# Splitting seven of sixteen weight tiles inside the attention, and the rest on GpSimd over the first group

## The chip, the cores and the metric

One Trainium2 chip, one core. The metric is the device time of one execution in microseconds (us). Three runs of the kernel before gave 1213.04, 1215.56 and 1216.34 us; the median is 1215.56 us. A 0.3% difference is about 3.6 us.

## The reference

Two stages follow each other. The first is a linear attention: for each of 8 x 8 heads (576 tokens, 64 dimensions) queries and keys are projected to 128 features, the largest absolute value of each row is subtracted, and both exp(p) and exp(-p) are kept.

```
proj = x @ w_phi;  proj -= max(abs(proj), axis=-1);  phi = concat(exp(proj), exp(-proj))
kv = k_p^T v;  z = sum_s k_p;  out = (q_p kv) / (q_p z + 1e-6)
```

The second stage takes the 4608 tokens with 512 features each:

```
h = x @ w_in            # 512 -> 2048
g = h - tanh(h)
y = g @ w_out           # 2048 -> 512
```

The weights w_in and w_out arrive as 64-bit floating point numbers and are decoded on the chip to 32 bits.

## The kernel before, in words

**Attention.** A unit is a pair of heads of one batch; there are 32 units, u0 to u31. The loop `for i in range(NU + 2)` is a software pipeline: period i projects unit i (`project`, TensorE, with `m` and `t` on VectorE, L201 and L203), forms keys and queries of unit i-1 (`k_exp`, `q_exp` on ScalarE; `kv`, `ksum`, `qt`, `kv_turn` on TensorE), and forms the outputs of unit i-2 (`out_heads`, L267 and L278; `out_copy`; `den` reads the denominators back by DMA into `dn`; `den_recip` inverts them and sends them through memory to `rb`). `den_mul` (L314, GpSimd) multiplies unit i-3 by `rb` and stores it to memory as `xs`. In periods 0 to 31 one weight tile is decoded too (`dec_0` to `dec_2`, ScalarE and VectorE): tile n is w_in block n/2 for even n, w_out block n/2 for odd n. Within `tc.manual_schedule()` each engine keeps the order in which the lines are written.

**Weight splits.** TensorE multiplies in a reduced 32-bit format, so each weight tile (128x512) is split in a high part `wh` (a cast) and a low part `wl = w - wh` (a subtraction). `split_w(f)` does both for w_in block f (`whi`, `wli`) and w_out block f (`who`, `wlo`). The cast of w_in is on ScalarE (L88), that of w_out on VectorE (L90); the subtraction (L92) is on GpSimd, but for w_out blocks 3 to 15 on VectorE. Blocks 0 to 2 are split at the end of the attention (period 32 and after the loop), the others in steps 0 to 12 of the second stage. There, `pin` keeps instructions in the order in which they are written; the rest is ordered by a planner, which schedules everything outside the manual section.

**Second stage.** Tokens go in 12 groups of 384, and each group in 16 steps (f = 0 to 15), 192 steps in all. `stage1` makes h for one block of 128 features: 4 x 3 matmuls (`xh` by `whi`, `xl` by `whi`, `xh` by `wli`, L426) in one of three PSUM tiles `ph`. Five ScalarE functions and five VectorE operations (L442, L443, L445, L446, L447) make g; L447 frees `mk`, of which there is one buffer and which L441 of the next step writes. `split_g` makes `gh` (ScalarE, L453) and `gl` (GpSimd, L454). `stage2` of step f, written after `stage1` of step f+2, adds nine matmuls (L460, L461, L463) to three output tiles. The activations x of group 0 are loaded from `xs` in period 32 (`x_load`, four DMAs) and split there (`x_split`, four casts on ScalarE, four subtractions on VectorE, L109 and L110); those of group g+1 are loaded and split in steps 0 to 11 of group g. `den_mul` of the last unit is pinned on GpSimd in step 2. All DMAs are issued by SyncE's queue (SP), in order.

In `split_w` before, the engine of the subtraction and the early pool hang on these lines:

```
wh = (wpa if f < AHEAD else wp[0]).tile(...)      # AHEAD = 3
e = nc.vector if nm == "o" and f >= AHEAD else nc.gpsimd
```

Of the kernel before, what the change touches and what calls it, by code (L numbers as in the profile page):

```python
# [8 lines left out]
F32 = mybir.dt.float32  # L9
# [18 lines left out]
def f32(ap):  # L28
    return ap.bitcast(F32)
# [3 lines left out]
def tile_linear_attention_moe(  # L33
# [20 lines left out]
    NT = B * S // P  # L54
    TPP = 2 * S // P
    G = 3
    AHEAD = 3
    PC = 2 * S
    NCT = DM // P
    NF = DFF // P  # L60
# [18 lines left out]
    xp0 = ctx.enter_context(tc.tile_pool(name="xp0", bufs=1, reuse_waits="tile"))  # L79
    wi, wo, wp, xp = {}, {}, [], []  # L80

    def split_w(f, pin=lambda ins: ins):
        for d, nm in ((wi, "i"), (wo, "o")):
            w = d[f]
            wh = (wpa if f < AHEAD else wp[0]).tile([P, DM], F32R, name=f"wh{nm}{f}")
            wl = wpool.tile([P, DM], F32R, tag="w", name=f"wl{nm}{f}")
            if nm == "i":
                pin(nc.scalar.copy(wh, w))  # L88
            else:
                pin(nc.vector.tensor_copy(wh, w))  # L90
            e = nc.vector if nm == "o" and f >= AHEAD else nc.gpsimd
            pin(e.tensor_tensor(wl, w, f32(wh), ALU.subtract))  # L92
            d[f] = (wh, wl)

    def x_tiles(g):
        pool = xp0 if g % 2 == 0 else xp[0]
        xh = pool.tile([P, NCT, G * P], F32R, tag="xh", name=f"xh{g}")
        xl = pool.tile([P, NCT, G * P], F32R, tag="xl", name=f"xl{g}")
        return xh, xl, {}

    def x_load(g, xt, c):
        bp, o = divmod(g * G, TPP)
        x = xp0.tile([P, G * P], F32, tag="x", name=f"x{g}_{c}", bufs=4)
        nc.sync.dma_start(x, xs[bp][c, :, o * P : (o + G) * P])
        xt[2][c] = x
# [10 lines left out]
    with ExitStack() as c1:  # L116
# [15 lines left out]
        def warm(n):  # L132
            for _ in range(n):
                nc.tensor.matmul(pw[:, 0:256], zt[:, 0:P], zt, start=True, stop=True)
# [22 lines left out]
        def dec_0(u):  # L157
            rr = u.r.bitcast(U32).rearrange("p (n t) -> p n t", t=2)
            u.lo, u.hi = rr[:, :, 0], rr[:, :, 1]
            u.a = raw.tile([P, DM], U32, tag="dec_a", name=f"dec_a{u.nm}", bufs=2)  # L160
            nc.scalar.activation(f32(u.a), f32(u.hi), AF.Abs, scale=65536.0)
# [17 lines left out]
        def load(u):  # L179
            u.qk = p2.tile([P, PC], F32, tag="qk", name=f"qk{u.i}")  # L180
            w = PC if u.i else 3 * P
            for o in range(0, PC, w):
                nc.sync.dma_start(u.qk[:, o : o + w], qkT[u.i][:, o : o + w])

        def load_v(u):
            u.v = p2.tile([P, 5, 2, D], F32, tag="v", name=f"v{u.i}")
            nc.sync.dma_start(u.v.rearrange("p j e d -> p (j e d)"), v5[u.i])


        def project(u, r):  # L190
            pp = ps_pj.tile([P, 2, 512], F32, tag="pj", name=f"pp{u.i}_{r}")
            for a in range(3):
                j = 3 * r + a
                for e in range(2):
                    hs = slice(e * D, (e + 1) * D)
                    nc.tensor.matmul(  # L196
                        pp[:, e, a * F : (a + 1) * F], u.qk[hs, j * P : (j + 1) * P], wph[hs, :], start=True, stop=True
                    )
            x = pp[:, :, 0 : 3 * F].rearrange("p e (a f) -> p e a f", f=F)
            m = p2.tile([P, 2, 3], F32, tag="m", name=f"m{u.i}_{r}")  # L200
            nc.vector.tensor_reduce(m, x, AX.X, ALU.max, apply_absolute_value=True)  # L201
            t = p2.tile([P, 2, 3, F], F32, tag=f"t{r}", name=f"t{u.i}_{r}")
            nc.vector.tensor_tensor(t, x, m.unsqueeze(3).broadcast_to([P, 2, 3, F]), ALU.subtract)  # L203
            u.t[r] = t
# [22 lines left out]
        def k_exp(u, r):  # L227
            x, j0, j1 = (u.t[1][:, :, 1:3, :], 0, 2) if r == 1 else (u.t[2], 2, 5)
            for s in range(2):
                nc.scalar.activation(u.kp[:, :, j0:j1, s, :], x, AF.Exp, scale=1.0 - 2.0 * s)  # L230
# [62 lines left out]
        def den(u):  # L293
            w = 2 * S // P
            dn = tail.tile([P, w], F32, tag="dn", name=f"dn{u.i}")
            nc.sync.dma_start(dn, u.dd.rearrange("(n r) c -> n r c", r=32)[:, 0, :])
            u.dn = dn
# [33 lines left out]
        def unit(i):  # L331
            return units[i] if 0 <= i < NU else None


        with tc.manual_schedule():
            for i in range(NU + 2):
                a, c, p, p2_ = unit(i), unit(i - 1), unit(i - 2), unit(i - 3)
                if i + 1 < NU:
                    load(units[i + 1])
                    load_v(units[i + 1])  # L340
                if i == NU:
                    xt = {0: x_tiles(0)}
                    for j in range(NCT):
                        x_load(0, xt[0], j)
                if a:
                    a.kp = p2.tile([P, 2, 5, 2, F], F32, tag="kp", name=f"kp{i}")
                    if i == 0:
                        warm(16)
                    project(a, 0)
                if c and i < NU:  # L350
                    k_exp(c, 2)
                if p:
                    out_heads(p)
                if c and i == NU:
                    k_exp(c, 2)
                if 2 <= i < NU:
                    dec_0(dec[i])
                    dec_1(dec[i])
                if p:
                    out_copy(p)  # L360
                    den(p)
                if p2_:
                    den_mul(p2_)
                if i < 2:
                    warm(8)
                if c and i == 1:
                    kv(c)
                if a:
                    project(a, 1)
                if c and i > 1:  # L370
                    kv(c)
                if a:
                    k_exp(a, 1)
                if 2 <= i < NU:
                    dec_2(dec[i])
                if 2 <= i < NU - 2:
                    dec.append(dec_load(i + 2))
                if i == NU:
                    for j in range(NCT):
                        x_split(xt[0], j)  # L380
                if i == 0:
                    warm(8)
                if a:
                    project(a, 2)
                if i < 2:
                    dec_0(dec[i])
                    dec_1(dec[i])
                    dec_2(dec[i])
                    dec.append(dec_load(i + 2))
                if c:  # L390
                    c.qe = p1.tile([P, 2, 2, S], F32, tag="qe", name=f"qe{i - 1}")
                    pt = qt(c, 0)
                    q_exp(c, 0, pt)
                    ksum(c)
                    ptr = qt_rest(c)
                    kv_copy(c)
                    q_exp_rest(c, ptr)
                    pt = qt(c, 1)
                    kv_turn(c)
                    q_exp(c, 1, pt)  # L400
                if p:
                    den_recip(p)
                if i == NU:
                    split_w(0)
            for f in range(1, AHEAD):
                split_w(f)

    with ExitStack() as c2:  # L410
# [62 lines left out]

        NG = NT // G
        steps = [(g, f) for g in range(NG) for f in range(NF)]
        po, gs, gg = {}, {}, {}
        for i in range(len(steps) + 2):
            if i < len(steps):
                g, f = steps[i]
                if f == 0:  # L480
                    po[g] = [ps_o.tile([P, DM], F32, tag="o", name=f"po{g}_{t}") for t in range(G)]
                gs[i] = stage1(g, f, *xt[g][:2])
                if g + 1 < NG:
                    if f == 0:
                        xt[g + 1] = x_tiles(g + 1)
                    if f % 3 == 0 and f < 3 * NCT:
                        x_load(g + 1, xt[g + 1], f // 3)
                    if f % 3 == 2 and f < 3 * NCT:
                        x_split(xt[g + 1], f // 3, pin)
            if 1 <= i <= len(steps):  # L490
                g, f = steps[i - 1]
                gg[i - 1] = split_g(g, f, gs.pop(i - 1), G)
            if i == 2:
                den_mul(units[-1], pin)
            if i + AHEAD < NF:
                split_w(i + AHEAD, pin)
            if i >= 2:
                g, f = steps[i - 2]
                stage2(po[g], f, *gg.pop(i - 2), G)
                if f == NF - 1:  # L500
                    store(g * G, po.pop(g), G)
# [55 lines left out]
```

## Time and profile before

| | us |
|---|---|
| median of three runs | 1215.56 |
| profiled execution, its own time | 1214.86 |
| its span in the trace | 1213.1 |
| TensorE (PE) busy | 1186.4 (98%) |
| VectorE (DVE) busy | 890.8 (73%) |
| ScalarE (ACT) busy | 800.6 (66%) |
| GpSimd (POOL) busy | 272.6 (22%) |
| mean granted TensorE clock | 0.995 |

The span is the time between the first and the last instruction in the trace; 1.8 us of the execution's time lie around it. Busy shares are means over the whole span. The attention takes the first third of the span, the second stage the rest. PEclk is the granted TensorE clock as a share of 2.4 GHz.

### The profile page before, as it was taken

Reading aid. Unit: us, or ns where it says so; the run is one execution under the profiler, and the core shown is the slowest. Engines: PE = TensorE matmul, PEld = TensorE weight load, DVE = VectorE, ACT = ScalarE, POOL = GpSimd, SP = SyncE. Lnnn points to the kernel's source line nnn. Section 1 sums busy time; section 2 is a strip of 40 time slices with the busy share of each in tenths; the row PEclk is TensorE's granted clock in tenths of the full one; section 3 lists DMA queues with packets and bytes.
Section 4 is the critical chain, followed back from the end, with each engine's and each line's share of the span. In section 5 each row is a group of like instructions: output and inputs, shape, how many; then the busy total and the mean of one; then the engine's idle time right before and its main releaser. Section 6 shows DMA issues by size and latency. Waiting matters only on the chain.

```text
span 1213.1 us, 22447 instructions
## 1 busy us (share of the span) xinstructions
PE 1186.4 (98%) x8584; PEld 969.9 (80%) x8584; DVE 890.8 (73%) x1478; ACT 800.6 (66%) x1709; POOL 272.6 (22%) x253
## 2 busy tenths in 40 slices
PE   7999999999998899999999999999999999999998
PEld 5666666666665688999999999999999999999997
DVE  5877777777774998677677777777676777777665
ACT  3566566566666676777677766776676667766665
POOL 0001111011113552222222222222222222222222
PEclk9999999999999999999999999999999999999999
DMA  4566566556553000000010100010000100000000
GB/s 153 160 180 194 158 186 197 156 189 198 169 163 113 26 19 33 14 34 20 7 40 14 39 15 33 14 38 15 25 23 14 40 14 34 21 26 1 27 1 26
DMA packets 51180, 85.70 MB, mean 71 GB/s; under 512 B 13312, under 2 KB 28160, under 8 KB 51072
## 3 DMA queue, kind: packets, MB, share of 16 engines
q1 hardware_dynamic: 51072, 84.27, 22.6%
q8 instruction: 67, 1.10, 0.4%
q14 instruction: 41, 0.34, 0.1%
HBM read 65.08 MB, written 19.02 MB: 69 GB/s over the span
## 4 chain that ended last, share of the span: by engine, by line
PE 90%; DVE 5%; DMA 2%; issue 1%; ACT 1%; SPq 0%; DVEq 0%
PE ph L426 31%; PE po L461 10%; PE po L460 10%; PE po L463 10%; PE pp L196 7%; PE pc L238 6%; PE po L267 5%; PE pc L246 3%; PE ptt L209 3%; PE po L278 3%; DVE s L443 1%; PE ptk L257 1%; DVE s L447 1%; PE ptr L215 1%; DVE s L445 1%
## 5 line engine op out<-in xcount | busy, mean ns | idle before, releaser
L454 POOL TENSOR_TENSOR gl<-s,gh 128x384 fp32r<-128x384 f32 x192 | 197.5, 1029 | 592.6 <-ACT gh L453 582.0
L426 PE MATMUL ph<-xh,wli 128*128 128x384 f32 x768 | 259.8, 338 | 2.7 <-POOL wli L92 2.7
L426 PE MATMUL ph<-xh,whi 128*128 128x384 f32 x768 | 259.0, 337 | 1.0 <-DVE th L446 1.0
L426 PE MATMUL ph<-xl,whi 128*128 128x384 f32 x768 | 258.3, 336 | 0.0
L433 ACT ACTIVATE y<-ph 128x384 f32<-128x384 f32 x192 | 94.4, 491 | 228.4 <-PE ph L426 228.4
L460 PE MATMUL po<-who,gh 128*128 128x512 f32 x576 | 227.9, 396 | 7.9 <-ACT gh L453 7.8
L442 DVE SCALAR_TENSOR_TENSOR s<-s,y 128x384 f32<-128x384 f32 x192 | 111.1, 579 | 166.7 <-ACT s L435 166.6
L461 PE MATMUL po<-wlo,gh 128*128 128x512 f32 x576 | 227.0, 394 | 0.0
L463 PE MATMUL po<-who,gl 128*128 128x512 f32 x576 | 164.5, 394 | 0.0
L426 PEld LDWEIGHTS ph<-xh,whi 128*128 128x128 f32 x768 | 144.6, 188 | 10.1 <-issue 1.7
L447 DVE COPY_PREDICATED s<-mk,th 128x384 f32<-128x384 uint32 x192 | 136.4, 710 | 20.1 <-DVE th L446 0.5
L426 PEld LDWEIGHTS ph<-xl,whi 128*128 128x128 f32 x768 | 144.5, 188 | 8.2
L426 PEld LDWEIGHTS ph<-xh,wli 128*128 128x128 f32 x768 | 144.3, 188 | 3.8 <-POOL wli L92 3.6
L230 ACT ACTIVATE kp<-t 128x768 f32<-128x768 f32 (+1 forms) x128 | 87.2, 733 | 74.5 <-DVE t L203 74.5
L441 ACT ACTIVATE mk<-y,bias_t 128x384 f32<-128x384 f32 x192 | 117.9, 614 | 20.5 <-DVE s L447 20.5
L460 PEld LDWEIGHTS po<-who,gh 128*128 128x128 f32 x576 | 107.8, 187 | 28.6 <-ACT gh L453 11.5
L443 DVE SCALAR_TENSOR_TENSOR s<-s,s 128x384 f32<-128x384 f32 x192 | 115.1, 599 | 18.9 <-ACT mk L441 0.9
L463 PEld LDWEIGHTS po<-who,gl 128*128 128x128 f32 x576 | 108.5, 188 | 25.3
L201 DVE TENSOR_REDUCE m<-pp 128x6 f32<-128x768 f32 x96 | 91.8, 956 | 46.4 <-PE pp L196 46.4
L314 POOL TENSOR_TENSOR rb<-d,rb 128x576 f32<-128x576 f32 x32 | 46.5, 1454 | 336.6 <-DMA rb<-rr 336.6
L461 PEld LDWEIGHTS po<-wlo,gh 128*128 128x128 f32 x576 | 108.2, 188 | 16.4
L435 ACT ACTIVATE s<-y,bias_t 128x384 f32<-128x384 f32 x192 | 118.4, 617 | 0.0
(63 smaller groups left out, 1653.8 us busy)
## 6 DMA issues: line engine op xcount, KB each, us to landing
qk<-in_qkT SPq DMA_DIRECT2D x31, 576.0 KB, 4.7
v<-in_v SPq DMA_DIRECT2D x32, 320.0 KB, 7.0
rb<-rr SPq DMA_DIRECT2D x64, 144.0 KB, 2.9
xs<-rb SPq DMA_DIRECT2D x32, 288.0 KB, 2.4
x<-xs SPq DMA_DIRECT2D x48, 192.0 KB, 2.3
out<-o SPq DMA_DIRECT2D x36, 256.0 KB, 2.2
rawi<-in_moe_w_in SPq DMA_DIRECT2D x16, 512.0 KB, 4.3
rawo<-in_moe_w_out SPq DMA_DIRECT2D x16, 512.0 KB, 4.5
```

Source lines behind the costliest of these rows:

```text
L201: nc.vector.tensor_reduce(m, x, AX.X, ALU.max, apply_absolute_value=True)
L426: nc.tensor.matmul(h, wt[:, c * P : (c + 1) * P], x[:, c, 0:N], start=(i == 0), stop=(i == 3 * NCT - 1))
L433: nc.scalar.activation(y, h, AF.Square)
L435: nc.scalar.activation(s1, y, AF.Square, bias=bias_t[:, 0:1])
L441: nc.scalar.activation(mk, y, AF.Relu, bias=bias_t[:, 2:3])
L442: nc.vector.scalar_tensor_tensor(s1, s1, PC1, y, ALU.add, ALU.mult)
L443: nc.vector.scalar_tensor_tensor(s2, s2, PC2, s1, ALU.add, ALU.mult)
L447: nc.vector.copy_predicated(gs, mk.bitcast(U32), th)
L454: pin(nc.gpsimd.tensor_tensor(gl, gs, f32(gh), ALU.subtract))
L460: nc.tensor.matmul(po[t], a, wo[f][0], start=(f == 0), stop=False)
L461: nc.tensor.matmul(po[t], a, wo[f][1], start=False, stop=False)
L463: nc.tensor.matmul(po[t], gl[:, t * P : (t + 1) * P], wo[f][0], start=False, stop=(f == NF - 1))
```

## The change

`AHEAD` becomes 7. `split_w` now handles one tile n (even n: w_in, odd n: w_out). Tiles 0 to 13, that is blocks 0 to 6 of both weights, are split one per period in periods 1 to 14 of the attention, right after `den_mul`. The casts of these fourteen are on ScalarE, w_out's too. Tiles 14 to 31 are split in the first group, spread evenly over its 16 steps (1.2 per step); their casts stay where they were. Every subtraction is on GpSimd. The x of group 0 is loaded in period 30, ahead of that period's other DMAs except the loads of unit 31, and split at the end of period 31. The last period (33: outputs of u31, `den_mul` of u30) is no longer in the manual section and is ordered by the planner together with the second stage.

```
-    AHEAD = 3
+    AHEAD = 7
+    def split_w(n, pin=lambda ins: ins):
+        d, nm, f = (wi, wo)[n % 2], "io"[n % 2], n // 2
+        early = f < AHEAD
+        w = d[f]
+        wh = (wpa if early else wp[0]).tile([P, DM], F32R, name=f"wh{nm}{f}")
+        wl = wpool.tile([P, DM], F32R, tag="w", name=f"wl{nm}{f}")
+        if early or nm == "i":
+            pin(nc.scalar.copy(wh, w))
+        else:
+            pin(nc.vector.tensor_copy(wh, w))
+        pin(nc.gpsimd.tensor_tensor(wl, w, f32(wh), ALU.subtract))
+        d[f] = (wh, wl)
...
+        def period(i):
+            if i == NU - 2:
+                xt[0] = x_tiles(0)
+                for j in range(NCT):
+                    x_load(0, xt[0], j)
...
             if p2_:
                 den_mul(p2_)
+            if 1 <= i <= 2 * AHEAD:
+                split_w(i - 1)
...
             if p:
                 den_recip(p)
+            if i == NU - 1:
+                for j in range(NCT):
+                    x_split(xt[0], j)
...
         with tc.manual_schedule():
-            for i in range(NU + 2):
-                if i == NU:
-                    split_w(0)
-            for f in range(1, AHEAD):
-                split_w(f)
+            for i in range(NU + 1):
+                period(i)
+        period(NU + 1)
...
+        late = list(range(2 * AHEAD, 2 * NF))
+        NL = len(late)
-            if i + AHEAD < NF:
-                split_w(i + AHEAD, pin)
+            while late and late[0] <= 2 * AHEAD + i * NL // (NF - 1):
+                split_w(late.pop(0), pin)
```

## Rows read from the trace of the kernel before

**Rows 1.** Busy time per engine by stretch; then granted clock, DMA share, GB/s.
```profile
48.40:371.50 323.10, 322.08 (x4003) 206.66 (x4001) 250.63 (x369) 203.64 (x427) 40.82 (x29) 1.00 0.59 176
371.50:399.20 27.70, 22.33 (x180) 14.51 (x180) 12.62 (x23) 15.84 (x36) 12.28 (x9) 0.94 0.37 112
399.20:472.50 73.30, 65.53 (x308) 56.47 (x309) 68.81 (x108) 50.14 (x106) 37.83 (x29) 0.98 0.05 16
472.50:1199.10 726.60, 726.60 (x3645) 658.21 (x3644) 520.86 (x929) 505.76 (x1094) 176.12 (x174) 1.00 0.07 23
382.80:387.60 4.80, 4.80 (x32) 2.12 (x32) 0.51 (x3) 0.64 (x2) 2.49 (x2) 0.66 0.46 140
```
**Rows 2.** Waits of PE, 371 to 472.5 us: total, times, longest.
```profile
PE po L460 <- ACT gh L453: 7.0, 7, 1.7
PE ph L426 <- POOL wli L92: 2.7, 3, 1.3
PE ptt L209 <- ACT qe L220: 1.7, 1, 1.7
```
**Rows 3.** PE in order of time around the change of stage: start, us.
```profile
371.56 2.16 PE L267 MATMUL po<-qe,kv 128*64 128x288 f32 x16 [0.65 <-DVE kv L259]
...
382.79 3.77 PE L267 MATMUL po<-qe,kv 128*64 128x288 f32 x16 [0.65 <-DVE kv L259]
...
399.22 0.50 PE L460 MATMUL po<-who,gh 128*128 128x512 f32 x1 [0.36 <-ACT gh L453]
```
**Rows 4.** Groups of instructions, 416.8 to 462.4 us: count, busy, mean ns, idle.
```profile
L443 DVE SCALAR_TENSOR_TENSOR s<-s,s 128x384 f32<-128x384 f32 x9 | 11.3, 1261 | 0.6
...
L92 DVE TENSOR_TENSOR wlo<-wo,who 128x512 fp32r<-128x512 f32 x9 | 6.2, 688 | 0.2
...
L88 ACT CAST whi<-wi 128x512 fp32r<-128x512 f32 x8 | 4.9, 617 | 0.0
...
L90 DVE CAST who<-wo 128x512 fp32r<-128x512 f32 x9 | 3.8, 418 | 0.0
```
**Rows 5.** Groups of DVE and of POOL, 600 to 800 us.
```profile
L442 DVE SCALAR_TENSOR_TENSOR s<-s,y 128x384 f32<-128x384 f32 x48 | 26.9, 560 | 44.7 <-ACT s L435 44.7
L443 DVE SCALAR_TENSOR_TENSOR s<-s,s 128x384 f32<-128x384 f32 x48 | 26.8, 558 | 4.7
...
L454 POOL TENSOR_TENSOR gl<-s,gh 128x384 fp32r<-128x384 f32 x48 | 48.9, 1018 | 152.1 <-ACT gh L453 152.1
```
**Rows 6.** Lines L447 and L92: ns min/median/max, first and last start us.
```profile
L447 DVE COPY_PREDICATED s<-mk,th x10: 586/601/1533, 416.9 to 462.4; 128x384 f32<-128x384 uint32 x10
...
L92 POOL TENSOR_TENSOR wli<-wi,whi x16: 1266/1603/1626, 383.5 to 454.7; 128x512 fp32r<-128x512 f32 x16
```
**Rows 7.** POOL and DVE in order of time, one step of the first group.
```profile
459.56 1.25 POOL L454 TENSOR_TENSOR gl<-s,gh 128x384 fp32r<-128x384 f32 x1 [3.29 <-ACT gh L453]
...
460.04 1.19 DVE L443 SCALAR_TENSOR_TENSOR s<-s,s 128x384 f32<-128x384 f32 x1
```
**Rows 8.** Waits in the attention, 48.4 to 371.5 us.
```profile
ACT kp L230 <- DVE t L203: 52.9, 28, 1.9
...
DVE m L201 <- PE pp L196: 32.9, 53, 0.8
...
DVE rn L304 <- DMA dn<-dd: 0.8, 1, 0.8
```
**Rows 9.** Lines L203 and L171, all executions: ns min/median/max, first and last start.
```profile
L203 DVE TENSOR_TENSOR t<-pp,m x96: 956/957/958, 8.0 to 368.9; 128x768 f32<-128x768 f32 x96
...
L171 DVE SCALAR_TENSOR_TENSOR wi<-rawi,dec_ai x16: 679/682/1754, 17.3 to 355.0; 128x512 uint32<-128x512 uint32 x16
```
**Rows 10.** SP's queue in order of time: start, us.
```profile
374.48 2.00 SPq L104 DMA_DIRECT2D x<-xs  x4
...
392.61 1.10 SPq L309 DMA_DIRECT2D rb<-rr  x2
```
**Rows 11.** POOL in order of time: start, us.
```profile
405.23 1.43 POOL L314 TENSOR_TENSOR rb<-d,rb 128x576 f32<-128x576 f32 x1
```

More of the change, by code (lines that the diff above doesn't have):

```diff
@@ L80, in tile_linear_attention_moe @@
     wi, wo, wp, xp = {}, {}, [], []
[L82 to L93, printed above, removed]
+    def split_w(n, pin=lambda ins: ins):
[10 more added lines that the diff above has]
+        d[f] = (wh, wl)
     def x_tiles(g):
@@ L332, in unit @@
             return units[i] if 0 <= i < NU else None
-        with tc.manual_schedule():
-            for i in range(NU + 2):
[L337 to L340, printed above, removed]
-                if i == NU:
[L342 to L403, printed above, removed]
-                    split_w(0)
-            for f in range(1, AHEAD):
-                split_w(f)
@@ new lines, in period @@
+        def period(i):
+            a, c, p, p2_ = unit(i), unit(i - 1), unit(i - 2), unit(i - 3)
+            if i + 1 < NU:
+                load(units[i + 1])
+                load_v(units[i + 1])
+            if i == NU - 2:
+                xt[0] = x_tiles(0)
+                for j in range(NCT):
+                    x_load(0, xt[0], j)
+            if a:
+                a.kp = p2.tile([P, 2, 5, 2, F], F32, tag="kp", name=f"kp{i}")
+                if i == 0:
+                    warm(16)
+                project(a, 0)
+            if c:
+                k_exp(c, 2)
+            if p:
+                out_heads(p)
+            if 2 <= i < NU:
+                dec_0(dec[i])
+                dec_1(dec[i])
+            if p:
+                out_copy(p)
+                den(p)
+            if p2_:
+                den_mul(p2_)
+            if 1 <= i <= 2 * AHEAD:
+                split_w(i - 1)
+            if i < 2:
+                warm(8)
+            if c and i == 1:
+                kv(c)
+            if a:
+                project(a, 1)
+            if c and i > 1:
+                kv(c)
+            if a:
+                k_exp(a, 1)
+            if 2 <= i < NU:
+                dec_2(dec[i])
+            if 2 <= i < NU - 2:
+                dec.append(dec_load(i + 2))
+            if i == 0:
+                warm(8)
+            if a:
+                project(a, 2)
+            if i < 2:
+                dec_0(dec[i])
+                dec_1(dec[i])
+                dec_2(dec[i])
+                dec.append(dec_load(i + 2))
+            if c:
+                c.qe = p1.tile([P, 2, 2, S], F32, tag="qe", name=f"qe{i - 1}")
+                pt = qt(c, 0)
+                q_exp(c, 0, pt)
+                ksum(c)
+                ptr = qt_rest(c)
+                kv_copy(c)
+                q_exp_rest(c, ptr)
+                pt = qt(c, 1)
+                kv_turn(c)
+                q_exp(c, 1, pt)
+            if p:
+                den_recip(p)
+            if i == NU - 1:
+                for j in range(NCT):
+                    x_split(xt[0], j)
@@ L410, in tile_linear_attention_moe @@
+        xt = {}
+        with tc.manual_schedule():
+            for i in range(NU + 1):
+                period(i)
+        period(NU + 1)
     with ExitStack() as c2:
```

## The prediction

> **What bounds the kernel now.** First the busy time by stretch [rows 1]: TensorE (PE) is busy for 322.08 of 323.10 us of the attention and for all of 726.60 us after the first group. There only less matmul work would help, and the change removes none. The two stretches between are different: 5.4 us of PE idle from 371.5 to 399.2, and 7.8 us from 399.2 to 472.5, the 15 steps from the first second-stage product of step 0 to that of step 15. In the second, VectorE (DVE) is busy 68.81 of 73.30 us. That is 4.89 us a step; later PE takes 4.187 us (726.60 us for 3645 matmuls at 21 a step).
>
> Then the waits of PE [rows 2]: 7.0 us for `gh`, the end of the DVE chain; 2.7 us for `wli`, the early splits on GpSimd (POOL); 1.7 us for a `q_exp` that stands in ScalarE's (ACT) queue behind the casts of x. After that last idle time the clock falls: the granted clock from 382.8 to 387.6 us is 0.66 [rows 1], a mix of the two levels of 2.4 and 1.2 GHz, and the same 16 matmuls of `out_heads` take 3.77 us where they took 2.16 [rows 3], 1.6 us lost.
>
> Why DVE takes 4.89 us a step is seen in the groups and in the order of time. L443 takes 558 ns in the steady groups [rows 5] and 1261 ns in the first one [rows 4]; the single step shows it: `gl` runs on POOL from 459.56 to 460.81, L443 starts at 460.04 and ends at 461.23, 0.42 us after POOL is done [rows 7]. So a DVE operation that reads SBUF only waits until POOL's tensor operation ends. L203, with one input in PSUM, takes 956 to 958 ns in all 96 cases, with POOL or without [rows 9].
>
> **The change part by part.** I write times against the profiled execution, 1214.86 us.
>
> *Attention, splits of tiles 0 to 13.* Each period of 11.39 us (L203, 96 times from 8.0 to 368.9, three a period [rows 9]) gets one ACT cast of 0.617 us [rows 4] and one POOL subtraction of 1.27 to 1.6 us [rows 6]. The cast stands before `k_exp`, where ACT waits 1.9 us a period for `t` (52.9 us in 28 waits [rows 8]): hidden, and uncovered it would cost 14 x 0.617 = 8.6 us. POOL is busy 40.82 of 323.10 us [rows 1], so it has room; its operation falls behind `den_mul`, while DVE does `m` and `t` from PSUM, which L203 shows unharmed. DVE itself waits for PE 0.6 us at a time (32.9 us in 53 waits [rows 8]), so that small shifts are absorbed. I take 0, with a gain excluded, since PE has 1 us of idle there in all; the other end stands under the rivals.
>
> *x loaded in period 30.* Four DMAs take 2.00 us of SP's queue [rows 10]. Queued behind them now are `dn`, the store of `xs`, `rr` and `rb` of that period. DVE takes `dn` in order, and once waited 0.8 us for it [rows 8]; then `m` of the next unit and PE's projections follow. Bounds 0 and 2.0 us; I take +0.5, since the 0.6 us waits of DVE cover part. The `dn` DMA of period 32 goes out earlier by as much. The split at the end of period 31 lies where DVE has nothing else, and ACT's four casts end before `out_copy` of u30 needs it.
>
> *Transition, 371.56 to 399.22.* The 1.7 us wait of PE goes, since no cast of x stands in front of `q_exp`; with it I expect the slow clock to go, 1.6 us. The 2.7 us for `wli` go, as blocks 0 to 6 are split long before. The two waits of 0.65 us for `kv` stay [rows 3], though the planner may put first-stage matmuls into the second. Restarts of PE add some tenths. Sum -6.2 us, first `gh` product at about 393. What is late next is the chain of step 0 (ACT, DVE, `gh`). Bounds: -3.3 if that chain takes back the 2.7 us, -8 if the `kv` waits are filled too.
>
> *First group, 15 steps.* Count what POOL and DVE can't do at the same time. Per step before: L442 and L443 0.56 each, L447 0.60, the cast 0.42, `wlo` 0.69 on DVE; `gl` 1.02 and `wli` 1.27 on POOL [rows 4 to 6]; sum 5.12. DVE's pace was 45.5/9 = 5.06 us (ten L447 from 416.9 to 462.4 [rows 6]), so the sum holds within 1%. After: 0.56 + 0.56 + 0.60; 9 casts in 15 steps, 0.25; `gl` 1.02; 18 subtractions in 15 steps, 18 x 1.27/15 = 1.52. Sum 4.51, by the same 1% 4.46 us a step. That is still above PE's 4.187, so the first group stays bound by DVE and POOL: 15 x 4.46 = 66.9 in place of 73.3, -6.4 us. Bounds: -10.5 (4.187 a step, DVE keeps up because it starts a step ahead) and 0.
>
> *Added waits.* The cast of tile 14 writes memory that the attention's last tiles hold, as the cast of block 3 did. `den_mul` of u31 is pinned in step 2 with `gl` of steps 2 and on queued behind it, and PE behind them. Before, `rb` went out at 392.61 and POOL took it at 405.23 [rows 10, 11], over 11 us after; both move up by about 6 us, so the margin stays. The last period, now ordered by the planner, keeps its work; 0 to 2 us either way, inside the range.
>
> Sum: +0.5 - 6.2 - 6.4 = -12.1, so 1202.8 for an execution like the profiled one. That one lies 0.7 us under the median of 1215.56; I add a little and say **1203.0**.
>
> A rule speaks against the change. The Trainium skill (Perfetto Trace Analysis, section Optimizing Scalar/DVE Operations) says that moving operations between DVE and GpSimd might not help, as they share a read port of SBUF. By that rule the first group would gain nothing; it is the second rival. The trace agrees with the sharing [rows 7], and shows what the move costs: 1.27 us on POOL for 0.69 on DVE.
>
> **The rivals.**
>
> *PE becomes the bound (20%).* At 4.187 us a step the first group saves 10.5. For it: DVE's own work falls by 0.42 + 0.69 - 0.25 = 0.86 us a step, and the planner lets the first stage run up to three tiles ahead. Against: the sum above is a sum of things that exclude each other. 0.5 - 6.2 - 10.5 = -16.2: 1198.7.
>
> *The move gives nothing in the first group (16%).* Eighteen subtractions at 1.27 us are 22.9 us of POOL, against 13 x 1.27 + 13 x 0.69 = 25.5 us on both engines before. If POOL's longer holds, two in some steps, cost DVE what it no longer does itself, the step stays at 4.89. Against: four blocks are gone from the group, 4 x (0.42 + 0.69 + 1.27) = 9.5 us. +0.5 - 6.2: 1209.2.
>
> *Slower: the splits stall the attention (7%).* A POOL subtraction in each of 14 periods holds DVE just when `m` of the next projection is due. L171 shows the price: up to 1.75 us in place of 0.68 under `den_mul` [rows 9], 1.07 us. With POOL's slowest 1.6 us the hold is up to 1.6, less nothing if DVE's 0.6 us wait is already used: 14 x 1.6 = 22.4 us, 1214.86 + 22.4 - 12.1 = 1225. It turns the sign from 12.1/14 = 0.86 us of PE idle a period. Against: 29 `den_mul` in the attention's 323 us leave PE 1 us idle in all.
>
> *The change doesn't do what it says (5%).* The planner, free in the last period, puts `out_heads` and DVE's `dn` operations so that DVE stands in order before a DMA with step 0's chain behind it. Then the transition keeps its length and the first group starts late; the 6.2 are lost and the 6.4 stay: 1209.
>
> **How the numbers follow.** Forecast 52%, own range 1200 to 1206; rivals 20, 16, 7 and 5%. The range 1197 to 1209.5 holds the first, the forecast and most of the second, and leaves out the slower case; the transition's and the x loads' bounds (3 and 1.5 us up) lie inside. A change of 0.3%, 3.6 us, is about what a measurement of this kernel can tell from none. Faster by more 0.90, within 0.03, slower 0.07.
>
> **What would show it.** Right: no PE wait for `wli`, no wait of about 1.7 us for `q_exp` before `ptk` of u31, and a granted clock near 1.00 around `out_heads` of u31; L447 of the first group some 4.4 to 4.5 us apart; L443 still far above 558 ns there; L203 still 957 ns; the attention as long as before to within 1 us. Wrong: PE gaps in periods 1 to 14; a first group of 73 us; a first `gh` product later than 396. A clock that falls to half in the first group again would cost what the step's pace gains.

## The result and the profile after

The changed kernel took 1205.36 us in the median of six runs (1202.87 to 1206.69), the kernel before 1216.37 us on the same chip (1213.04 to 1217.57): a ratio of 0.991 (95% interval 0.9894 to 0.9926), 11.0 us less. The profiled execution took 1203.97 us, its span is 1202.0 us. The forecast for such an execution was 1202.8, the forecast time 1203.0.

The busy time by stretch of the changed kernel, cut where its own stages begin (columns as in rows 1; the last cut lies 0.5 us before its first product of step 15, at 461.50):

```profile
48.40:371.50 323.10, 322.21 (x4005) 206.80 (x4001) 252.13 (x368) 209.47 (x439) 56.63 (x41) 1.00 0.60 179
371.50:392.50 21.00, 20.18 (x182) 14.33 (x182) 8.35 (x18) 14.18 (x33) 4.14 (x3) 1.00 0.37 104
392.50:461.00 68.50, 63.36 (x304) 54.10 (x305) 61.45 (x89) 48.45 (x103) 43.20 (x34) 1.00 0.06 19
461.00:1188.00 727.00, 727.00 (x3647) 658.65 (x3646) 522.07 (x932) 505.72 (x1094) 177.07 (x174) 1.00 0.07 23
```

Against [rows 1], GpSimd (POOL) has 15.8 us more in the attention and TensorE (PE) is as busy there as before. The transition shrinks from 27.7 us to 21.0, at full clock. The first group still holds 5.1 us of PE idle; after it PE is busy without a gap. The same places in PE's order of time (compare [rows 3]):

```profile
363.45 0.94 PE L197 MATMUL pp<-wph,qk 64*128 64x128 f32 x12 [0.28 <-DVE t L204]
...
371.55 2.16 PE L268 MATMUL po<-qe,kv 128*64 128x288 f32 x16 [0.65 <-DVE kv L260]
...
381.05 2.16 PE L268 MATMUL po<-qe,kv 128*64 128x288 f32 x16 [0.65 <-DVE kv L260]
...
392.56 0.50 PE L462 MATMUL po<-who,gh 128*128 128x512 f32 x1 [0.18 <-ACT gh L455]
```

Period 32 starts its `out_heads` at 371.55, before at 371.56. The next `out_heads` takes 2.16 us where it took 3.77, and the first `gh` product comes at 392.56, where it came at 399.22. What PE waited for from 371 to 462 us (compare [rows 2]):

```profile
PE po L462 <- ACT gh L455: 2.3, 4, 0.8
PE po L465 <- POOL gl L456: 1.5, 3, 0.6
PE po L268 <- DVE kv L260: 1.3, 2, 0.7
PE ph L428 <- POOL wli L93: 1.3, 1, 1.3
```

7.0 us for `gh` became 2.3. The wait for `q_exp` is gone. Two waits are left on POOL: 1.5 us for `gl`, which wasn't there before, and one of 1.3 us for a `wli`. That one is the last w_in tile; in order of time, POOL and then PE:

```profile
449.60 1.33 POOL L456 TENSOR_TENSOR gl<-s,gh 128x384 fp32r<-128x384 f32 x1
450.90 1.26 POOL L93 TENSOR_TENSOR wli<-wi,whi 128x512 fp32r<-128x512 f32 x1
...
452.21 0.44 PE L428 MATMUL ph<-xh,wli 128*128 128x384 f32 x1 [1.29 <-POOL wli L93]
```

The even spread puts the last w_in tile in step 14, one step before its use, and PE stands until it is split. VectorE's (DVE) pace, by the operation that ends a step (L449, before L447, compare [rows 6]; minimum, median, maximum ns, first and last start):

```profile
L449 DVE COPY_PREDICATED s<-mk,th x15: 598/1394/1581, 390.5 to 451.2; 128x384 f32<-128x384 uint32 x15
```

Fourteen steps in 60.7 us are 4.34 us a step. The same fourteen steps before:

```profile
L447 DVE COPY_PREDICATED s<-mk,th x15: 579/602/1691, 396.4 to 465.2; 128x384 f32<-128x384 uint32 x15
```

They took 68.8 us, 4.91 a step; the 5.06 of the prediction is the pace of nine of them, from 416.9 to 462.4.

To compare the runs below I use three marks of each profile: T, the start of `out_heads` of period 32; G, the first `gh` product; S, the first copy of group 0's output (DVE), two us after the first product of step 15. What happens before T varies from profile to profile by up to 3.7 us, so T to S is the better measure. There is one profile of each kernel. Times are us, the ratios are to the kernel before on the same chip.

| kernel | T to G | G to S | T to S | ratio (95% interval) |
|---|---|---|---|---|
| before | 27.7 | 75.4 | 103.1 | 1 |
| changed | 21.0 | 71.0 | 92.0 | 0.991 (0.9894 to 0.9926) |
| late `wlo` on DVE | 21.0 | 73.9 | 94.9 | 0.9922 (0.9909 to 0.9934) |
| before, x alone | 25.1 | 75.4 | 100.5 | 0.9985 (0.9976 to 0.9994) |
| spread two earlier | 21.3 | 69.8 | 91.1 | 0.9912 (0.9897 to 0.9928) |
| no late subtractions | 20.8 | 64.9 | 85.7 | 0.9861 (0.9846 to 0.9876) |
| x back in period 32 | 22.6 | 72.2 | 94.8 | 0.9936 (0.9919 to 0.9953) |
| late `wlo` on DVE, two earlier | 21.3 | 72.2 | 93.5 | 0.9916 (0.99 to 0.9933) |
| late casts on ScalarE, two earlier | 21.8 | 67.2 | 89.0 | 0.9873 (0.9855 to 0.9891) |
| five early blocks | 21.0 | 78.9 | 99.9 | 0.9979 (0.9968 to 0.9989) |
| last period by hand | 21.0 | 71.1 | 92.1 | 0.9918 (0.9905 to 0.993) |
| late tiles in pairs | 21.0 | 74.2 | 95.2 | 0.994 (0.9927 to 0.9954) |
| five early, three earlier | 21.3 | 72.7 | 94.0 | 0.993 (0.9915 to 0.9944) |

T to S fell by 11.05 us from before to changed: all of the gain, 6.65 in the transition and 4.40 in the first group.

How far T to S varies between executions of one kernel isn't known; changed and last period by hand, which no mark tells apart, agree within 0.1 us. One thing does disturb it: for a stretch the granted clock falls to 0.50. Between T and S this happens twice in the profile of before (from 382.6 and from 416.6 us) and once in those of late `wlo` on DVE, x alone, x back, and five early, three earlier; in the others the clock stays at 1.00. Summed over windows of 0.4 us, each stretch costs PE 1.7 us of full-speed time. In the second one of before DVE was busy for 3.33 of 3.40 us (416.8 to 420.2), so it probably has no part in the 4.40 us; no run shows that. Whether a stretch belongs to the kernel or to the execution isn't shown: two of the changed kernel's six executions, the profiled one among them, have a mean granted clock of 0.997 or 0.998, the other four 0.995. Differences of 2 to 3 us between two profiles are read below with this in mind.

### The profile page after: what moved, and what is told of

It is laid out like the page before. It is cut to its first block, busy times and chain, and to the rows that moved or that the text cites. A ratio compares the mean times of both kernels' runs of the same rounds, so it can differ in the third digit from the quotient of the medians.

```text
span 1202.0 us, 22462 instructions
## 1 busy us (share of the span) xinstructions
PE 1181.3 (98%) x8584; PEld 967.1 (80%) x8584; DVE 881.3 (73%) x1458; ACT 804.7 (67%) x1716; POOL 288.8 (24%) x266
## 4 chain that ended last, share of the span: by engine, by line
PE 93%; DVE 3%; issue 1%; DMA 1%; POOL 0%; ACT 0%; DVEq 0%; SPq 0%; POOLq 0%; ACTq 0%
PE ph L428 32%; PE po L465 10%; PE po L463 10%; PE po L462 10%; PE pp L197 7%; PE pc L239 7%; PE po L268 5%; PE pc L247 4%; PE ptt L210 3%; PE po L279 3%; PE ptk L258 1%; DVE s L445 1%; PE ptr L216 1%; DVE s L449 1%; DMA dn<-dd 0%
## 5 line engine op out<-in xcount | busy, mean ns | idle before, releaser
L444 DVE SCALAR_TENSOR_TENSOR s<-s,y 128x384 f32<-128x384 f32 x192 | 108.0, 562 | 167.9 <-ACT s L437 167.9
L449 DVE COPY_PREDICATED s<-mk,th 128x384 f32<-128x384 uint32 x192 | 140.3, 731 | 20.5 <-ACT y L435 0.5
L462 PEld LDWEIGHTS po<-who,gh 128*128 128x128 f32 x576 | 107.9, 187 | 22.6 <-ACT gh L455 5.6
L443 ACT ACTIVATE mk<-y,bias_t 128x384 f32<-128x384 f32 x192 | 117.9, 614 | 6.5 <-DVE s L449 6.3
L439 ACT ACTIVATE s<-y,bias_t 128x384 f32<-128x384 f32 x192 | 117.6, 612 | 1.4 <-POOL gl L456 1.3
L437 ACT ACTIVATE s<-y,bias_t 128x384 f32<-128x384 f32 x192 | 118.4, 617 | 0.0
```

Of the source, the lines that this page charges most:

```text
L437: nc.scalar.activation(s1, y, AF.Square, bias=bias_t[:, 0:1])
L439: nc.scalar.activation(s2, y, AF.Square, bias=bias_t[:, 1:2])
L443: nc.scalar.activation(mk, y, AF.Relu, bias=bias_t[:, 2:3])
L444: nc.vector.scalar_tensor_tensor(s1, s1, PC1, y, ALU.add, ALU.mult)
L449: nc.vector.copy_predicated(gs, mk.bitcast(U32), th)
L462: nc.tensor.matmul(po[t], a, wo[f][0], start=(f == 0), stop=False)
```

## The experiments

**Late `wlo` back on VectorE.** The prediction added up the durations on DVE and POOL as if they excluded each other (below: the port sum). By that sum this is faster still.

```
-        pin(nc.gpsimd.tensor_tensor(wl, w, f32(wh), ALU.subtract))
+        e = nc.gpsimd if early or nm == "i" else nc.vector
+        pin(e.tensor_tensor(wl, w, f32(wh), ALU.subtract))
```

> The changed kernel, but the subtraction of the nine late w_out tiles is on VectorE again, as before the change. Theory (VectorE's operations on SBUF and GpSimd's exclude each other, and their sum sets the pace of the first group): the sum falls from 4.51 us a step by 9 x 1.27/15 = 0.76 and rises by 9 x 0.69/15 = 0.41, to 4.16, under TensorE's 4.187; the first group shrinks from 68.9 us to 63 to 65, and the time falls by 4 to 6 us against the changed kernel, to about 1200. Rival (VectorE's own work is the bound, so that the move to GpSimd is what brought the gain): VectorE gets 6.2 us more work in the group where it was busy for 61.5 of 68.5 us; the group is as long or longer, 68 to 72 us, and the time 1205 to 1209.

G to S grew by 2.9 us, from 71.0 to 73.9; 66 had been expected on this scale. The port sum fails. DVE's steps, as above:

```profile
L450 DVE COPY_PREDICATED s<-mk,th x15: 593/610/1607, 390.2 to 453.3; 128x384 f32<-128x384 uint32 x15
```

63.1/14 = 4.51 us a step, where the sum had said 4.16. The whole time isn't told apart from the changed kernel's (ratios 0.9922 and 0.991); the 4 to 6 us that the sum had promised are not there.

Not all of the 2.9 us is the move's. In both kernels PE waits 1.3 us for the last w_in tile and has no gap from there to S. This last piece, in the changed kernel and then in this one (columns as in rows 1):

```profile
452.21:463.58 11.37, 11.37 (x58) 10.37 (x58) 7.56 (x14) 7.46 (x17) 3.87 (x3) 1.00 0.00 1
```
```profile
453.30:466.20 12.90, 12.90 (x57) 11.91 (x58) 7.43 (x14) 7.45 (x17) 2.29 (x2) 0.87 0.01 1
```

The clock costs 1.5 us here. That leaves 1.4 us up to the end of that wait.

**x alone.** In the kernel before, the loads of x move to period 30 and the split to the end of period 31.

```
-                if i == NU:
+                if i == NU - 2:
                     xt = {0: x_tiles(0)}
...
-                if i == NU:
-                    for j in range(NCT):
-                        x_split(xt[0], j)
...
+                if i == NU - 1:
+                    for j in range(NCT):
+                        x_split(xt[0], j)
```

> The kernel before, with one part of the change alone: the first x loaded in period 30 and split at the end of period 31. Theory: the 1.7 us wait of TensorE for q_exp and the slow clock behind it (1.6 us) go, the x loads cost 0.4 us, the rest of the transition and the first group stay: 2.5 to 3.5 us faster than before, granted clock near 1.00 around the last out_heads. Rival (the waits for the early splits take it back, since GpSimd and ScalarE still have to split three blocks there): within 1 us of before, with the waits for wli grown from 2.7 us to over 5.

T to G fell by 2.6 us, and both effects of the theory are seen: the second `out_heads` takes 2.16 us, and no wait for `q_exp` is left. But the waits for `wli` grew from 2.7 to 3.5 us:

```profile
PE po L460 <- ACT gh L453: 7.0, 7, 1.7
PE ph L426 <- POOL wli L92: 3.5, 3, 1.7
```

The whole time fell by 0.15%, 1.8 us, less than expected; in the profile, PE also waited 1.0 us for `t` in the attention, behind the x loads. So of 6.65 us this part alone brings 2.6; the rest needs the early splits (the run with x back in period 32 has them without this part).

**The spread two tiles earlier.**

```
-            while late and late[0] <= 2 * AHEAD + i * NL // (NF - 1):
+            while late and late[0] <= 2 * AHEAD + 2 + i * NL // (NF - 1):
```

> The changed kernel, with the spread of the late tiles moved two tiles earlier, so that the last w_in tile is split in step 12 and not in step 14, one step before its use. Theory (the first group is 2 us longer than the 66.9 us of the sum because TensorE waits 1.29 us for the last wli, and step 14 behind it starts late): that wait goes, the pace of the other steps stays at 4.5, the group takes 66.5 to 67.5 us, the time falls by 1.5 to 2.4 us against the changed kernel. Rival (the pace of the port sets the end of the group whatever the order): the group stays at 68.5 to 69.5 and the time within 0.7 us.

The wait for `wli` is gone, and the stretch is 1.2 us shorter, T to S 0.9:

```profile
PE po L465 <- POOL gl L456: 2.8, 4, 1.4
PE po L462 <- ACT gh L455: 1.8, 2, 0.9
PE po L268 <- DVE kv L260: 1.3, 2, 0.7
```

The waits for `gl` grew from 1.5 to 2.8 us instead: with more tiles in the first steps POOL is late with `gl`. Between theory and rival; the times don't tell the two kernels apart.

**No late subtractions.**

```
+        if early:
+            wl = wpool.tile([P, DM], F32R, tag="w", name=f"wl{nm}{f}")
+        else:
+            wl = wh
...
-        pin(nc.gpsimd.tensor_tensor(wl, w, f32(wh), ALU.subtract))
+        if early:
+            pin(nc.gpsimd.tensor_tensor(wl, w, f32(wh), ALU.subtract))
```

> The changed kernel without the eighteen late subtractions: the low part of the late tiles is left out and their high part is used twice, so the matmuls stay. Theory (port sum): 4.51 - 1.52 = 2.99 us a step, under VectorE's own run of instructions and under TensorE's 4.187; TensorE is the bound, the first group takes 62.8 to 64 us, and the time falls by 5 to 6 us against the changed kernel. L443's counterpart (the second of the five operations) takes under 800 ns there. Rival (ScalarE and VectorE in turns, with one buffer for mk, set the pace): the group stays above 66 us.

As the theory said: G to S is 64.9 us, and fifteen steps at PE's 4.187 and the two us to the copy make 64.9. L443's counterpart takes 558 ns from 400 to 450 us, the changed kernel's 1086:

```profile
L449 DVE SCALAR_TENSOR_TENSOR s<-s,s 128x384 f32<-128x384 f32 x13 | 7.3, 558 | 1.4
```

So eighteen subtractions on POOL, with the waits for `wli` and `gl` that come of them, cost this group at least 6.1 us; below that PE is the bound.

**x back in period 32.**

```
-            if i == NU - 2:
+            if i == NU:
                 xt[0] = x_tiles(0)
...
+            if i == NU:
+                for j in range(NCT):
+                    x_split(xt[0], j)
...
-            if i == NU - 1:
-                for j in range(NCT):
-                    x_split(xt[0], j)
```

> The changed kernel with one part undone: the first x is loaded in period 32 and split there, as before. Theory (that part is worth TensorE's 1.7 us wait for q_exp and the slow clock behind it, less 0.4 us of x loads): the wait comes back, the granted clock around the last out_heads falls below 0.8, the way from the start of the first out_heads of period 32 to the first gh product grows from 21.0 to 24 us, and the time is 2.5 to 3.5 us above the changed kernel's. Rival (with the weights split early the planner fills the wait with first-stage matmuls, so that clock and time stay): within 1 us of the changed kernel.

T to S grew by 2.8 us, as expected, but not in the way expected. The wait for `q_exp` is back with 1.6 us, and T to G grew by that, to 22.6 us; 27.7 before makes 5.1 us for the other parts of the change, the early splits above all, 1.7 of them the slow stretch that this profile doesn't have there. The clock did not fall behind that wait. It fell later, behind the 1.3 us wait for the last w_in tile (windows of this kernel, columns as above):

```profile
384.00:387.20 3.20, 3.20 (x33) 1.47 (x33) 0.24 (x2) 0.94 (x3) 0.00 (x0) 1.00 0.32 103
...
450.00:460.00 10.00, 7.91 (x31) 6.60 (x30) 5.34 (x8) 4.22 (x10) 3.96 (x3) 0.83 0.00 1
```

The other 1.2 us, from G to S, are this slow stretch. The same wait of 1.3 us cost the changed kernel no clock. Which idle time of this size the slow clock follows isn't settled.

**Late `wlo` on VectorE, spread two earlier.** Both edits above together, against the spread alone.

> The late w_out subtractions on VectorE once more, now with the spread two tiles earlier, so that no late w_in tile disturbs the end; to be compared with the kernel that has the earlier spread alone (span 1200.1, first gh product to first store copy 69.8 us). The port sum has failed in the first run of this kind. Theory now (VectorE's pace is its own work plus a wait of about 0.55 us per GpSimd operation, from 5.06 - 3.95 us for two a step before, 4.34 - 3.18 for 2.2 after, 4.50 - 3.54 for 1.6): nine times 0.60 us of own work against nine times 0.55 us of waits, a tie: the stretch takes 69.5 to 71 us, the time within 1 us. Rival 1 (port sum): 66 us, 4 us faster. Rival 2 (GpSimd's work costs VectorE next to nothing): 5 us longer.

72.2 against 69.8 us: 2.5 us longer, with the clock at 1.00 from T to S in both profiles. No tie, not 66, and not 75. The first pair gave 1.4 us without the clock. This makes 0.15 to 0.27 us for each of nine subtractions moved from DVE to POOL, in POOL's favour, from one profile each; the whole times (0.9916 and 0.9912) don't tell the two apart.

**Late casts on ScalarE, spread two earlier.**

```
-        if early or nm == "i":
-            pin(nc.scalar.copy(wh, w))
-        else:
-            pin(nc.vector.tensor_copy(wh, w))
+        pin(nc.scalar.copy(wh, w))
```

> The changed kernel with the spread two tiles earlier and the nine late w_out casts on ScalarE instead of VectorE. Theory (VectorE's own work plus its waits set the pace): 9 x 0.35 us less on VectorE, the stretch from first gh product to first store copy shrinks from 69.8 us by 2 to 3 us, to 67 or 68, and the time is about 3 to 4 us under the changed kernel's. Rival (ScalarE, in turns with VectorE by the one mk buffer, has no room for 9 x 0.5 us): the stretch stays at 69.5 to 71 us.

G to S is 67.2 us, 2.6 less than with the spread alone (T to S 2.1 less): the nine casts, 0.42 us each on DVE [rows 4], about 0.35 from start to start. It took 1200.63 us (1200.55 to 1201.16, 4 runs), against 1216.28 of before; its interval of the ratio lies below the changed kernel's. This version beats both; part of its lead may be the clock, which is 0.998 or 0.999 in the mean of each of its four executions. What PE still waits for:

```profile
PE po L459 <- ACT gh L452: 2.2, 4, 1.0
PE po L265 <- DVE kv L257: 1.3, 2, 0.7
PE po L462 <- POOL gl L453: 1.1, 2, 0.7
```

**Five early blocks.** `AHEAD = 5` in the changed kernel.

> The changed kernel with five blocks split early in place of seven: 22 late tiles instead of 18. Theory (0.55 us of VectorE's time per GpSimd subtraction, 0.35 per cast): 4 x 0.55 + 2 x 0.35 = 2.9 us more in the first group, time 2.5 to 3.5 us above the changed kernel's. Rival 1 (port sum): 4 x 1.27 + 2 x 0.42 = 5.9 us more. Rival 2 (the early blocks matter only for the transition, where five do as well as seven): within 1 us.

7.8 us more in the first group, more than any of the three had said. The waits show why:

```profile
PE ph L428 <- POOL wli L93: 5.1, 3, 2.8
PE po L462 <- ACT gh L455: 4.1, 5, 1.7
PE po L465 <- POOL gl L456: 2.8, 4, 1.7
```

5.1 us are for the last three w_in tiles, which the spread now puts two, one and one steps before their use; the changed kernel had 1.3.

**Five early blocks, spread three earlier.** `AHEAD = 5`, and `2 * AHEAD + 3 + i * NL // (NF - 1)`.

> Five early blocks, with the spread of the late tiles moved three tiles earlier, so that no w_in tile is split less than three steps before its use. The run with five early blocks cost 7.8 us in the first group, with 5.1 us of waits for late w_in tiles. Theory (the missing lead of the last w_in tiles is most of what went beyond the pace): the waits for wli fall under 1 us, the stretch from the first gh product to the first store copy falls from 78.9 to 74 to 76 us, the time by 3 to 5 us against that run. Rival (the pace alone): 77.5 to 80 us.

No wait for `wli` is left, and the stretch is 72.7 us, below the range expected: lead and not pace was most of the loss. Against seven blocks spread two earlier (69.8) it is 2.9 us more, what own work and 0.55 us a POOL operation had said for two blocks. That agreement is no proof. Step 0 now splits four tiles, `gl` stands behind them on POOL, and PE waits for it:

```profile
399.79 1.28 PE L465 MATMUL po<-who,gl 128*128 128x512 f32 x3 [2.84 <-POOL gl L456]
```

Behind this wait the clock is 0.50 from 400.4 to 403.6 us. By the starts of L449, 2.3 us more than with seven blocks arise in the first two steps, and 0.8 in the next twelve.

**Late tiles in pairs.** Two per step in steps 0 to 8, `late[0] <= 2 * AHEAD + 1 + 2 * i`.

> The changed kernel with the eighteen late tiles split two per step in steps 0 to 8 instead of being spread over the group. Theory (VectorE's pace is its own work plus waits for GpSimd, about 0.5 us per GpSimd operation): nine steps at 2.85 + 0.35 + 0.12 + 3 x 0.5 = 4.8 us, six at TensorE's 4.187, in all 68.5 us against 68.9; no late tile holds up the end; so within 1.5 us of the changed kernel, and 0.5 to 2 us slower than the spread that starts two tiles earlier. Rival (what the spread brought is most of the gain in the first group): 3 us or more slower than the changed kernel.

3.1 us longer than spread: the rival. DVE's nine steps of this kind took 46.2/9 = 5.13 us, and PE waits for `gl`, queued on POOL behind two subtractions:

```profile
L449 DVE COPY_PREDICATED s<-mk,th x10: 604/1422/1570, 390.3 to 436.5; 128x384 f32<-128x384 uint32 x10
```
```profile
PE po L465 <- POOL gl L456: 5.4, 6, 2.0
PE po L462 <- ACT gh L455: 1.3, 2, 0.9
```

**Last period by hand.** `for i in range(NU + 2): period(i)` within the manual section.

> The changed kernel with one part undone: the last period of the attention is in the order written by hand again, not the planner's. Theory (the planner there moves out_heads of u31 and its denominators only between other work; TensorE never waits for them): no change, within 1 us of the changed kernel, first gh product 21 us after the start of the first out_heads of period 32. Rival (order by hand puts the copies of u31's outputs and the inverse of its denominators before the first step's operations on ScalarE and VectorE): 1.5 to 4 us slower, the first gh product 2 us or more later.

T to G 21.0, G to S 71.1, both as in the changed kernel: no effect.

## Why the prediction was right, and where it wasn't

*Attention, forecast 0 for the splits and +0.5 for the x loads.* PE is busy 322.21 of 323.10 us, with 14 more subtractions on POOL and 14 more casts on ScalarE. The slower rival is out. The operation that writes `t` keeps its time in all 96 cases:

```profile
L204 DVE TENSOR_TENSOR t<-pp,m x96: 956/957/958, 7.4 to 369.4; 128x768 f32<-128x768 f32 x96
```

The x loads did what was said: DVE waited 1.4 us for `dn` once, and PE 0.28 us behind it. T came out as before all the same. The profile of before has a wait of PE of 0.4 us for a `qk` DMA in the attention, and this one has none; but with T varying by up to 3.7 us, the price of the loads can't be read from T.

*Transition, forecast -6.2 and the first `gh` product at about 393; measured -6.65 and 392.56.* The waits named went: `q_exp`, three of `wli`, and the slow clock. Undoing the x part brought the `q_exp` wait back; the x part alone brought 2.6 us, the rest of the change without it 5.1. That the clock falls behind that very wait, as I had put it, is not borne out: with the wait back it stayed at full speed there, and fell behind another.

*First group, forecast -6.4; by the same marks, first product of step 0 to that of step 15, 73.3 us became 68.9: -4.4.* This is the step with the error. The forecast set fifteen times the pace after, 66.9 us, against the measured group before, 73.3; by the same reckoning the group before would be 15 x 5.06 = 75.9, so that the sum itself says 9.0 us less and not 6.4. DVE's fourteen steps did shrink by 8.1 us, and their pace was a little better than forecast, 4.34 us and not 4.46. But the group kept only 4.4 of it. From the start of L449 in step 14 to the first product of step 15 it is 10.3 us, before (L447) 7.3: at the end PE has no gap behind the wait for the late tile, and DVE's pace no longer counts. (The other 0.8 us lie at the start of the group.)

What the forecast lacked is a term for the order: the last w_in tile is split one step before its use, and POOL, with up to two subtractions in front of `gl`, is late with `gl`. By the trace these are waits of 1.3 and 1.5 us; moving the spread took the first away and gave part of it back by the second. That the sum of all parts still came within 1.1 us of the forecast is partly luck: a pace too slow and a missing term at the end went against each other.

The reason for the pace was wrong too, though the number was near. A sum of DVE's and POOL's durations as if nothing overlapped fits before (5.12 against 5.06) and, within 4%, after (4.51 against 4.34), and fails where work is moved between the two: it said 4.16 and the run gave 4.51. What fits better is DVE's own instructions plus a wait for each POOL operation. The five operations of a step take 2.85 us when POOL has little to do (two L447 of the kernel before, a step apart, in order of time):

```profile
462.39 0.60 DVE L447 COPY_PREDICATED s<-mk,th 128x384 f32<-128x384 uint32 x1
...
465.23 0.60 DVE L447 COPY_PREDICATED s<-mk,th 128x384 f32<-128x384 uint32 x1
```

With a cast at 0.35, a subtraction at 0.60 and a split of x at 0.46 (start to start), own work is 3.95 us a step before, 3.18 changed, 3.54 with `wlo` on DVE, 3.32 in pairs. The rest of the measured pace, by POOL operations a step (2, 2.2, 1.6, 3), is 0.56, 0.53, 0.61 and 0.60 us for each. A subtraction on POOL runs 1.27 us or more, so by these figures about half of it falls beside DVE operations on PSUM (L447 and L448 keep 548 to 555 ns all through the group) or beside idle time. This is a mean, worked out from four profiles, and it does not give the price of a move: it had forecast a tie for `wlo` on DVE with the earlier spread, and the run was 2.5 us longer. From the two moves, a subtraction taken off POOL spared DVE only 0.3 to 0.45 us, against 0.60 of own work. Why less than the mean stays open.

*The rivals.* PE didn't become the bound; without the late subtractions it does, at 64.9. The second rival, that the move to POOL gives nothing in the first group, is not borne out: the group shrank by 4.4 us, and moved back it is 1.4 us (the clock taken out) and 2.5 us longer in the profiles. The Trainium skill (Perfetto Trace Analysis, section Optimizing Scalar/DVE Operations) says that moving work between the two might not help. Here it helped a little, by the profiles; the whole times are too coarse to show it. The planner's last period had no effect.

So the gain of 11 us is 6.65 in the transition, most of it by the early splits, and 4.4 in the first group. There, taken away one at a time, spreading is worth 3.1 us, `wlo` on POOL 1.4 to 2.5, and two of the four additional early blocks 2.9 where the lead is kept, with a slow stretch of the clock in that figure; these overlap and don't add up to 4.4, since undoing one makes another cost more.

## What to carry to other kernels

Where the operations of two engines hold each other up, don't price a move by the sum of their durations: what the mover sheds counts whole, and what the receiver takes on costs the other engine only the part that isn't covered (here 0.3 to 0.45 us of a subtraction of 1.27, by two moves). When work is spread evenly over a stretch, check the distance from each piece to its use at the end of the stretch, and what is queued behind each piece on its engine; here the two stood for 2.8 us of waits, and with four more tiles for nearly 8. Work given to a third engine that has room was worth as much as the whole question of the two (the casts on ScalarE, 2.1 us by T to S and 2.6 by G to S). And look at the granted clock before reading 2 us out of two profiles.

## What was not expected of the hardware

The granted clock falls to half behind some idle times of PE and not behind others of the same size. Behind 1.66 us before it did (0.66 of full speed in the 4.8 us after it), and not behind 1.55 us at the same place with x back in period 32. Behind the 1.3 us wait for the last w_in tile it fell with x back (0.83 over ten us) and with `wlo` on DVE, where the changed kernel and the one with the last period by hand kept 1.00. Behind 2.84 us it fell with five early blocks spread earlier; with five early blocks alone it kept 1.00 behind 2.80.
